# Slot logits one iteration later, and the copies of the transposed x ahead of the copies of the scores

## The chip, the cores and the metric

One core of a Trainium2 chip runs the whole program. The metric is the device time of one execution in microseconds (us), median over the runs; lower is better.

## The reference, cut to what matters

Three layers follow one another: windowed attention with four sink tokens, a soft mixture of experts, and a dense layer with the activation h - tanh(h).

```python
B, H, S, D = 4, 8, 768, 64              # 4 batches, 8 heads, 768 tokens
scores = q @ k.T / sqrt(D)              # kept where key < 4 or 0 <= i - j < 128
a = exp(scores - max); a /= sum(a) + 1e-9
x = concat over heads of (a @ v)        # 3072 x 512
logits = x @ phi                        # 3072 x 32 slots
d = softmax of logits over the tokens   # dispatch
c = softmax of logits over the slots    # combine
slot_input = d.T @ x                    # 32 x 512
slot_out = per expert: relu(slot_input @ w1[e]) @ w2[e]     # 8 experts
y = c @ slot_out
h = y @ w_in; out = (h - tanh(h)) @ w_out
```

## The kernel before

The order of all instructions is written out by hand: each engine runs its own queue in the order in which the program emits. The program has three parts: a software-pipelined loop over attention, a drain that finishes attention and the dispatch sums, and then the experts and the dense layer, whose order a planner works out from estimated costs. Only the first two parts are touched.

**The loop.** Its iterations i = 0 to 47 stand for 4 batches b, 4 pairs of heads p and 3 parts m (i % 3) of four score tiles each. An iteration holds work of several stages at once. In the order of emission:

- x_task (L655) transposes two thirds or one third of an earlier pair's output on TensorE (L434, tile mi) and leaves its copy back to SBUF in the list held.
- trans(i - 4) (L731) transposes the normalised scores (tile pT), and VectorE multiplies them by masks (L741 to L749).
- exps(i - 2) (L696): ScalarE takes four exponentials with their sums (L702).
- conv_step: a conversion of weights on VectorE, ScalarE (L130) and GpSimd, in part of the iterations.
- do_logits (L796): the slots' logits of a pair of heads, six matmuls x phi (L449, tile mi) and one VectorE operation that stores or adds them in ls (L452 for the first pair of a batch, L454 after that).
- scores(i) (L659): sixteen matmul records (L672) into two of the three buffers of tile sc.
- copies(i) (L675): ScalarE copies the scores to Z (L686), twice, or once where m is 0 (there VectorE does the other half, L683); VectorE overwrites masked parts (L687) and takes the maxima (L693).
- norm(i - 2) (L707): a VectorE reciprocal (L709) and a GpSimd multiply (L712).
- x_out (L651): ScalarE copies what held has (L436), so as to free the tile mi.
- run_task: a step of the dispatch sums of a finished batch (L463, L471, L502, L512, L521, L530, L535, each with a tile mi).
- avs(i - 5) (L751): the products with v (L767); where m is 2 ScalarE copies the result to xt (L781, L782), from which logits and transposes read.
- another run_task, and some DMA issues on SyncE.

Tile mi has two buffers, sc three, pT one, Z five. An entry for the logits falls due LD iterations after the avs that completes the pair, one for the transposes XD iterations after (and the second transposes no earlier than the iteration after the first). With LD = 1 the logits of a pair stand in the next iteration, i % 3 = 2; transposes stand in iterations of any remainder, since those of batches 1 and 2 wait until the dispatch sums of the batch before are done, and then one follows in each iteration.

**The drain** begins when the loop has ended. It clears the list lq, in which nothing is left, and then emits t_ext, trans, avs and the rest in an order given by the string DRAIN, the logits of the last two pairs under the names lg2 and lg3 among it. The weights of the experts are loaded by SyncE into buffers that the loop has used, so those loads are released by the last reads of the loop and the drain.

Of the kernel before, what the change touches and what calls it, by code (L numbers as in the profile page):

```python
# [44 lines left out]
NF = 0  # L45
ZO = 2
WT = (0, 0)
LD, XD, LP = 1, 2, 0
R78 = (41, 42)
NE_, NK = 12, 6  # L50
WF = (2, 0, 0, 0, 3, 0)
# [182 lines left out]
def tile_kernel(ctx: ExitStack, tc: tile.TileContext, qk, vv, v0, v0t, nw, phi, w1, w2,  # L234
# [17 lines left out]
    def run(ctx, fast):  # L252
# [49 lines left out]
        def win_src(i):  # L302
            d, f = divmod(i, 4)
            return w_in[P * d:P * d + P, 512 * f:512 * f + 512]
# [47 lines left out]
        def attention(fast):  # L352
            nqk = {}
            with ExitStack() as c2:
                ap = c2.enter_context(tc.tile_pool(name="ap", bufs=1))

                def load_qk(i):
                    a = sv(7 + i % 2, 0, QK)
                    SP.dma_start(a, qk[i // NP_, i % NP_])
                    nqk[i] = [a, None]  # L360
# [45 lines left out]
                def misc():  # L406
                    tag = seq.pop(0) if seq else "mi"
                    return pp.tile([P, 512], F32, name=tag, tag=tag, bufs={"mi": 2, "sc": 3, "pT": 1, "av0": 1}[tag])
# [35 lines left out]
                def logits(b, p):  # L444
                    if p == 0:
                        ls[b] = ap.tile([G3, 256], F32, name="ls", tag="ls", bufs=2)
                    m = misc()
                    for q in range(3):
                        PE.matmul(m[NS * q:NS * q + NS, 0:256], phi_t[:, p, :],  # L449
                                  xT[b, p][:, 256 * q:256 * q + 256], start=True, stop=True)  # L450
                    if p == 0:
                        DVE.tensor_copy(ls[b], m[0:G3, 0:256])  # L452
                    else:
                        DVE.tensor_tensor(ls[b], ls[b], m[0:G3, 0:256], op=ALU.add)  # L454
# [184 lines left out]
                steps, xq, lq = [], [], []  # L639
                cur = [[]]  # L640

                def next_step():
                    cur[0] = list(steps.pop(0)) if steps else []

                def run_task():
                    if cur[0]:
                        cur[0].pop(0)()
# [3 lines left out]
                def x_out():  # L651
                    while held:
                        held.pop(0)()

                def x_task():  # L655
                    if xq and not held and xq[0][0] <= now[0] and xq[0][1] <= done[0]:
                        xq.pop(0)[2]()
# [17 lines left out]
                def copies(i):  # L675
                    pb, m = divmod(i, 3)
                    Z = Zs[i]
                    for u in range(2):
                        s = sc_t[i][u]
                        z = Z[:, 2 * u:2 * u + 2, :]  # L680
                        base = bass.AP(s.tensor, s.offset, [list(s.ap[0]), [268, 2], [1, 132]])
                        if m == 0 and u == 0:
                            DVE.tensor_tensor(z, base, c_t[:, C_AB:C_AB + 264].rearrange("p (a c) -> p a c", a=2),  # L683
                                              op=ALU.add)
                        else:
                            ACT.copy(z, base)  # L686
                            DVE.copy_predicated(bass.AP(z.tensor, z.offset, [list(z.ap[0]), [196, 2], [1, 64]]),  # L687
                                                c_t[:, C_CM:C_CM + 128].bitcast(U32).rearrange("p (a c) -> p a c", a=2),
                                                bass.AP(s.tensor, s.offset + 132, [list(s.ap[0]), [68, 2], [1, 64]]))
                        if m == 0 and u == 1:  # L690
                            DVE.tensor_tensor(z[:, 0, 128:132], s[:, 128:132], c_t[:, C_C:C_C + 4], op=ALU.add)
                    mx = ap.tile([P, 4], F32, name="mx", tag="mx", bufs=4)
                    DVE.tensor_reduce(mx, Z, axis=AX.X, op=ALU.max)  # L693
                    small[i] = mx
# [36 lines left out]
                def trans(i, tag="pT"):  # L731
                    Z = Zs.pop(i)
                    pt = pp.tile([P, 512], F32, name=tag, tag=tag, bufs=1 if tag == "pT" else 3)
                    for u in range(4):
                        PE.transpose(pt[:, P * u:P * u + P], Z[:, u, 0:P], ident)  # L735
                    pb, m = divmod(i, 3)
                    src = pt.rearrange("p (t c) -> p t c", t=2)
                    mL, mU = (bass.AP(c_t.tensor, c_t.offset + o, [list(c_t.ap[0]), [0, 2], [1, 256]])
                              for o in (C_ML, C_MU))
                    if m == 0:  # L740
                        DVE.tensor_tensor(lu(0)[:, 256:512], pt[:, 256:512], mU[:, 0, :], op=ALU.mult)  # L741
                    elif m == 1:
                        d = sv(10, 512, 1024).rearrange("p (t l c) -> p t l c", t=2, l=2)
                        DVE.tensor_tensor(d[:, :, 1, :], src, mU, op=ALU.mult)
                    else:
                        for t in range(2):
                            DVE.tensor_tensor(lu(3 + t)[:, 256:512], src[:, t, :], mU[:, t, :], op=ALU.mult)
                    d = (sv(10, 1024 * m, 1024) if m < 2 else sv(11, 0, 1024)).rearrange("p (t l c) -> p t l c", t=2, l=2)
                    DVE.tensor_tensor(d[:, :, 0, :], src, mL, op=ALU.mult)  # L749
# [46 lines left out]
                def do_logits():  # L796
                    if lq and lq[0][0] <= now[0]:
                        logits(*lq.pop(0)[1:])


                def filler(s, n):
                    for _ in range(n):
                        PE.matmul(s[:, 400:512], z_t[:, 0:P], z_t[:, 0:112], start=True, stop=True)  # L803
# [29 lines left out]
                for i in range(NQ):  # L833
                    now[0] = i
                    next_step()
                    k = i - LAG
                    x_task()
                    if k >= 0:
                        trans(k)
                    k -= 1  # L840
                    if i >= 2:
                        exps(i - 2)
                    while stage[0] < min(3 * NC + 1, (i - 2) * CVR):
                        conv_step(stage[0])
                        stage[0] += 1
                    if LP == 0:
                        do_logits()
                    scores(i)
                    if i < NQ - 3:
                        filler(sc_t[i][1], NE_ if i < NK else NF)  # L850
                    copies(i)
                    if i == NQ - 1:
                        exps(NQ - 2)
                    if LP == 1:
                        do_logits()
                    if i % 3 == 2:
                        pre_dma = i // 3 + 2
                        if pre_dma < B * NP_:
                            load_qk(pre_dma)
                        else:  # L860
                            ring_dma(pre_dma - B * NP_ + 10)
                    if i >= 2:
                        norm(i - 2)
                    for b in range(B - 1):
                        if i in (12 * b + 14, 12 * b + 15):
                            sinks(b, (i % 12 - 2,))
                            break
                    else:
                        if gq:
                            gq.pop(0)()  # L870
                    if i == NQ - 1:
                        exps(NQ - 1)
                        norm(NQ - 2)
                    x_out()
                    if i < NQ - 1:
                        run_task()
                    if k >= 0:
                        avs(k)
                        if k % 3 == 2 and k // 3 + 2 < B * NP_:
                            load_v(k // 3 + 2)  # L880
                    run_task()
                    if i % 3 == 1 and pre:
                        ring_dma(pre.pop(0))
                    if i % 3 == 0 and i // 3 < 16 - NC:
                        SP.dma_start(late_raw(NC + i // 3), win_src(NC + i // 3))
                    for j, w in zip((5, 6), R78):
                        if i == w:
                            issued.add(j)
                            ring_dma(j)
# [16 lines left out]
                def warm_(n):  # L906
                    t = pp.tile([P, 512], F32, name="pT", tag="pT", bufs=1)
                    for _ in range(n):
                        PE.matmul(t[:, 0:ZN], z_t[:, 0:P], z_t, start=True, stop=True)

                lq.clear()
                t_ext, t_slota, t_slotb, t_slots, t_slotc = late2
                t_pst, t_sink, t_max, t_exp, t_trd, comb_max, t_ext2, t_trl, comb_sum, s_part, s_acc = tail_tasks(B - 1)[0]
# [1062 lines left out]
```

## Time and profile before

| what | value |
|---|---|
| median of 3 runs | 507.75 us (507.4 to 510.46) |
| the profiled execution | 508.94 us |
| its span, first to last instruction | 507.0 us |
| mean granted TensorE clock | 0.994 |
| TensorE busy | 480.7 us, 95% |
| VectorE busy | 414.6 us, 82% |
| ScalarE busy | 385.9 us, 76% |
| GpSimd busy | 301.6 us, 59% |

So 1.94 us of the profiled execution lie outside the span, and it is 1.19 us over the median. Shares are means over parts with different limits.

### The profile page before, as it was taken

Reading aid. Unit: us, or ns where it says so; the run is one execution under the profiler, and the core shown is the slowest. Engines: PE = TensorE matmul, PEld = TensorE weight load, DVE = VectorE, ACT = ScalarE, POOL = GpSimd, SP = SyncE. Lnnn points to the kernel's source line nnn. Section 1 sums busy time; section 2 is a strip of 40 time slices with the busy share of each in tenths; the row PEclk is TensorE's granted clock in tenths of the full one; section 3 lists DMA queues with packets and bytes.
Section 4 is the critical chain, followed back from the end, with each engine's and each line's share of the span. In section 5 each row is a group of like instructions: output and inputs, shape, how many; then the busy total and the mean of one; then the engine's idle time right before and its main releaser. Section 6 shows DMA issues by size and latency. Waiting matters only on the chain.

```text
span 507.0 us, 10286 instructions
## 1 busy us (share of the span) xinstructions
PE 480.7 (95%) x3558; PEld 336.7 (66%) x3558; DVE 414.6 (82%) x826; ACT 385.9 (76%) x1084; POOL 301.6 (59%) x366
## 2 busy tenths in 40 slices
PE   8799999899998999798999999999999999999995
PEld 4565655555555633235688888888888888888884
DVE  2999998998998559659999999788858798965892
ACT  4889998998999414337898987998768998855750
POOL 0466755765654100005899998358747794789871
PEclk9999999999999999899999999999999999999998
DMA  8989976532385999994433000220000030100022
GB/s 298 414 332 349 348 300 244 178 132 95 106 296 185 307 313 404 410 406 154 124 100 109 1 0 2 83 84 1 1 0 0 2 125 1 41 2 0 1 85 87
DMA packets 22139, 77.60 MB, mean 153 GB/s; under 512 B 2882, under 2 KB 4034, under 8 KB 20162
## 3 DMA queue, kind: packets, MB, share of 16 engines
q1 hardware_dynamic: 22082, 76.89, 41.4%
q8 instruction: 29, 0.48, 0.4%
q14 instruction: 28, 0.23, 0.1%
HBM read 70.59 MB, written 6.29 MB: 152 GB/s over the span
## 4 chain that ended last, share of the span: by engine, by line
PE 66%; DVE 10%; ACT 10%; DMA 8%; POOL 3%; issue 2%; DVEq 0%; POOLq 0%; SPq 0%; ACTq 0%
PE o L1507 44%; DMA w<-in_w 4%; ACT w L702 4%; PE sc L672 3%; PE o L1088 3%; PE av L767 2%; DMA w<-in_qk 2%; PE h L1576 2%; ACT w L686 2%; DVE mx L693 2%; DMA w<-in_w_out 2%; PE pT L735 2%; DVE w L749 1%; PE mi L530 1%; POOL gl L1320 1%
## 5 line engine op out<-in xcount | busy, mean ns | idle before, releaser
L1507 PE MATMUL o<-gh,whi 128*128 128x512 f32 x232 | 91.2, 393 | 0.0
L1507 PE MATMUL o<-gh,wlo 128*128 128x512 f32 x232 | 90.9, 392 | 0.0
L712 POOL TENSOR_TENSOR w<-w,su 128x528 f32<-128x528 f32 x38 | 40.6, 1068 | 52.4 <-DVE su L709 37.5
L1507 PE MATMUL o<-gl,whi 128*128 128x512 f32 x232 | 71.6, 390 | 0.0
L1499 POOL TENSOR_TENSOR gl<-w,gh 128x512 fp32r<-128x512 f32 x39 | 51.3, 1322 | 26.5 <-ACT gh L1645 15.5
L702 ACT ACTIVATE w<-w,nb 128x132 f32<-128x132 f32 x152 | 59.6, 393 | 1.2
L1507 PEld LDWEIGHTS o<-gh,whi 128*128 128x128 f32 x232 | 43.7, 188 | 9.9 <-ACT mk L1705 0.2
L1507 PEld LDWEIGHTS o<-gh,wlo 128*128 128x128 f32 x232 | 43.6, 188 | 9.7
L1507 PEld LDWEIGHTS o<-gl,whi 128*128 128x128 f32 x232 | 43.6, 188 | 9.5
L767 PE MATMUL av<-w,w 128*64 128x256 f32 (+1 forms) x448 | 48.3, 344 | 0.0
L672 PE MATMUL sc<-w 64*64 64x200 f32 (+2 forms) x768 | 44.8, 331 | 2.3 <-DMA w<-in_qk 1.4
L1147 POOL TENSOR_SCALAR whi<-wx 128x512 fp32r<-128x512 f32 x6 | 3.7, 619 | 62.8 <-DMA w<-in_w_out 61.0
L767 PEld LDWEIGHTS av<-w,w 128*64 128x64 f32 x448 | 25.8, 136 | 16.4 <-issue 10.7
L672 PEld LDWEIGHTS sc<-w 64*64 64x64 f32 x768 | 26.1, 132 | 15.1 <-issue 9.9
L1334 DVE TENSOR_TENSOR h<-u,h 128x512 f32<-128x512 f32 x40 | 27.6, 691 | 10.0 <-ACT u L1588 9.9
L1645 ACT CAST gh<-h 128x512 fp32r<-128x512 f32 x40 | 23.6, 590 | 11.1 <-DVE w L1499 4.2
L749 DVE TENSOR_TENSOR w<-pT,c_t 128x512 f32<-128x512 f32 x46 | 31.3, 680 | 0.0
L1645 ACT CAST gh<-w 128x512 fp32r<-128x512 f32 x39 | 24.2, 621 | 7.9 <-PE o L1507 7.6
L686 ACT COPY w<-sc 128x264 f32<-128x264 f32 x63 | 21.1, 373 | 11.9 <-PE sc L803 6.1
L1499 DVE TENSOR_TENSOR gl<-h,gh 128x512 fp32r<-128x512 f32 x40 | 27.4, 685 | 2.7 <-ACT gh L1645 2.0
L702 ACT ACTIVATION_READ_ACCUMULATOR w<-w,nb 128x1 f32 x152 | 28.3, 186 | 0.0
L693 DVE TENSOR_REDUCE mx<-w 128x4 f32<-128x528 f32 x38 | 26.7, 703 | 1.3
(388 smaller groups left out, 1332.2 us busy)
## 6 DMA issues: line engine op xcount, KB each, us to landing
w<-in_w SPq DMA_DIRECT2D x30, 512.0 KB, 10.2
w<-in_w SPq DMA_DIRECT2D x14, 1024.0 KB, 6.5
w<-in_qk SPq DMA_DIRECT2D x16, 780.0 KB, 6.1
w<-in_w_out SPq DMA_DIRECT2D x16, 512.0 KB, 3.6
w<-in_vv SPq DMA_DIRECT2D x16, 384.0 KB, 4.0
w<-in_w_in SPq DMA_DIRECT2D x8, 512.0 KB, 4.8
out<-xt SPq DMA_DIRECT2D x12, 256.0 KB, 2.0
win_t<-in_w_in SPq DMA_DIRECT2D x4, 512.0 KB, 9.5
```

The lines of the kernel that those rows point to most:

```text
L672: PE.matmul(sc_t[i][u][w, o:o + n], a[r, 64 * j:64 * j + 64], kslc(a, lo, n)[r, :], start=True, stop=True)
L686: ACT.copy(z, base)
L693: DVE.tensor_reduce(mx, Z, axis=AX.X, op=ALU.max)
L702: ACT.activation(Z[:, u, :], Z[:, u, :], AF.Exp, bias=nb[:, u:u + 1], scale=SCALE, accum_out=su[:, u, :])
L712: (POOL if i < NQ - 1 else DVE).tensor_tensor(Z, Z, su.to_broadcast([P, 4, CH]), op=ALU.mult)
L749: DVE.tensor_tensor(d[:, :, 0, :], src, mL, op=ALU.mult)
L767: PE.matmul(dst[r, :], v[:, t, r], l, start=start, stop=stop, skip_group_check=True)
L1088: PE.matmul(ha[x][NS * g:NS * g + NS, :], sT[f // 2][:, f % 2, :], ring_t(i + g, o, 512), start=f == 0, stop=f == 3)
L1334: DVE.tensor_tensor(g, u, h, op=ALU.mult)
L1499: td.any_of(at, {e: (us[e], lambda e=e: names[e].tensor_tensor(dst, a, b, op=alu), len(engs) > 1 or sbuf) for e in engs}, rd, wr)
L1507: PE.matmul(o, w, a, start=start, stop=stop)
L1645: add(at, "ACT", US["cast"], [gn], [f"gh{x}"], lambda: ACT.copy(gh_b[x], g))
```

## The change

Four edits. LD goes from 1 to 2: the logits of a pair are computed one iteration later, at i % 3 = 0 instead of 2. The call of x_out moves from behind norm and sinks to the place in front of copies, so that ScalarE's queue holds the copy of the transposed x ahead of the copies of the scores of the same iteration. As the pair (3, 1) is now due after the last iteration, a loop in front of lq.clear() computes what lq still holds for pairs under 2, at the head of the drain. Nothing else differs.

```diff
-LD, XD, LP = 1, 2, 0
+LD, XD, LP = 2, 2, 0
...
                     if i < NQ - 3:
                         filler(sc_t[i][1], NE_ if i < NK else NF)
+                    x_out()
                     copies(i)
...
                     if i == NQ - 1:
                         exps(NQ - 1)
                         norm(NQ - 2)
-                    x_out()
                     if i < NQ - 1:
                         run_task()
...
+                for a in lq:
+                    if a[2] < 2:
+                        logits(*a[1:])
                 lq.clear()
```

## Rows read from the trace of the kernel before

**Rows 1.** Stretches of the run: each engine's busy time (instructions), granted clock, DMA share, GB/s

```profile
29.00:163.00 134.00, 125.83 (x1495) 76.79 (x1494) 123.63 (x328) 126.58 (x547) 83.92 (x121) 1.00 0.63 229
163.00:182.00 19.00, 18.45 (x202) 11.44 (x202) 11.46 (x33) 8.55 (x28) 3.66 (x13) 1.00 0.90 318
182.00:196.00 14.00, 13.61 (x124) 4.25 (x128) 9.97 (x21) 3.21 (x5) 0.00 (x0) 1.00 0.96 335
196.00:228.00 32.00, 27.69 (x201) 10.61 (x197) 21.18 (x41) 12.61 (x24) 0.00 (x0) 0.95 1.03 408
```

**Rows 2.** Shorter stretches of the loop, the same columns

```profile
29.00:56.00 27.00, 25.54 (x297) 15.92 (x296) 25.16 (x67) 26.43 (x117) 18.66 (x25) 1.00 0.87 322
...
83.00:99.00 16.00, 14.82 (x176) 9.24 (x173) 15.71 (x40) 15.71 (x67) 10.35 (x20) 1.00 0.46 141
...
146.00:163.00 17.00, 15.24 (x186) 9.18 (x177) 15.22 (x42) 16.08 (x71) 6.54 (x11) 1.00 0.59 202
```

**Rows 3.** The chain that ended last, in order of time: start, length, what

```profile
129.08 0.56 PE mi L449 x6
...
130.56 0.66 ACT w L686 x2
131.22 0.50 ACT x L436
131.76 0.44 PE mi L434 x2
...
138.47 1.67 ACT w L702 x8
...
157.90 0.42 DVE w L687 x2
...
196.28 10.94 DMA w<-in_w
```

**Rows 4.** Waits, 15 to 172 us: who for whom, us in total, times, longest

```profile
DVE w L687 <- ACT w L686: 4.5, 11, 0.7
...
PE mi L449 <- ACT xt L781: 1.7, 3, 0.7
...
PE mi L512 <- ACT x L436: 1.3, 2, 0.9
PE mi L434 <- ACT x L436: 0.7, 1, 0.7
```

**Rows 5.** The instructions of one line, with their durations in ns

```profile
L436 ACT COPY x<-mi x24: 371/482/603, 34.3 to 154.1; 128x512 f32<-128x512 f32 x12, 128x256 f32<-128x256 f32 x12
...
  PE sc L434: 2.1, 1
  PE pT L434: 0.3, 1
```

**Rows 6.** The timeline at four places: start, duration, engine, line, idle before

```profile
99.56 0.58 DVE L687 COPY_PREDICATED w<-c_t,sc 128x128 f32<-128x128 uint32 x2 [0.68 <-ACT w L686]
99.70 0.39 ACT L436 COPY x<-mi 128x256 f32<-128x256 f32 x1
99.96 0.23 ACT L698 ACTIVATE nb<-mx 128x4 f32<-128x4 f32 x1
...
113.59 0.20 PEld L512 LDWEIGHTS mi<-c_t,ls 96*128 96x128 f32 x2 [1.36 <-ACT x L436]
...
130.56 0.66 ACT L686 COPY w<-sc 128x264 f32<-128x264 f32 x2 [0.40 <-PE sc L672]
...
154.27 0.30 DVE L687 COPY_PREDICATED w<-c_t,sc 128x128 f32<-128x128 uint32 x1 [0.39 <-ACT w L686]
```

**Rows 7.** The end of the loop, VectorE and ScalarE

```profile
160.16 0.66 ACT L686 COPY z<-sc 128x264 f32<-128x264 f32 x2 [0.25 <-PE sc L672]
...
160.22 0.41 DVE L454 TENSOR_TENSOR ls<-ls,mi 96x256 f32<-96x256 f32 x1
160.57 0.58 DVE L687 COPY_PREDICATED z<-c_t,sc 128x128 f32<-128x128 uint32 x2
```

## The prediction

> **What bounds the kernel now.** I read the busy times by stretch first, since the shares of the whole run mix three parts. In the loop, from 29 to 163 us, three engines are near full at once: of 134.00 us ScalarE is busy 126.58, TensorE 125.83, VectorE 123.63 [rows 1]. So none has more than some 10 us to give back, and ScalarE, the fullest, has 134.00 - 126.58 = 7.42 us. In two stretches it is the bound by itself: 26.43 of 27.00 us from 29 to 56, and 15.71 of 16.00 from 83 to 99 [rows 2]. There no order of its queue can gain more than 0.57 and 0.29 us.
>
> Second, the chain that ended last, which tells whose wait ends last at each place. It runs through ScalarE in those two stretches, through TensorE at 129 to 132 us, through VectorE near the loop's end, and at 196 us it steps into a transfer of weights [rows 3]. From 163 to 182 us, the drain, TensorE is busy 18.45 of 19.00 us; from 196 to 228 us the DMA engines are full, a share of 1.03 at 408 GB/s [rows 1]. Those transfers go to buffers that loop and drain set free, and the stream still has gaps from 163 to 182 us (a share of 0.90), so an earlier end of the loop moves the whole stream; a gain made only after 182 us would not.
>
> Third, the waits. The change can end three sorts of TensorE idle time: logits that wait for ScalarE's copy of the pair's output, 1.7 us, and matmuls that wait for a copy of x out of tile mi, 1.3 and 0.7 us [rows 4]; in all 3.7 us in the loop. Against them stands one wait that the change can lengthen: VectorE's masked overwrite waits for ScalarE's copy of the scores, 4.5 us in 11 places [rows 4].
>
> **The change, part by part.** No instruction is added or removed. What moves: 24 copies of x, twelve of four blocks and twelve of two, 371 to 603 ns each [rows 5], and the logits of 14 pairs, six matmuls and one VectorE operation each. The four-block copy holds up ScalarE's queue by 0.50 us [rows 3]; the two-block copy by 99.96 - 99.70 = 0.26 us, the time to the start of its successor [rows 6]. Neither part issues a DMA. The copies of x pass only copies of scores on ScalarE's queue; the logits pass one iteration's scores, products and maxima on TensorE's and VectorE's queues; GpSimd's and SyncE's queues stay as they are.
>
> *Logits one iteration later.* In the chain at 129 to 132 us logits of 0.56 us stand right in front of scores for which ScalarE has idled 0.40 us [rows 3, 6]. Moved, they let the scores end 0.56 us earlier, of which ScalarE can take the 0.40 us in which it sat idle: **-0.40 us**. They come back in the next iteration, in front of its scores; ScalarE has an iteration's exponentials, 1.67 us [rows 3], to take before it wants those, so I cost the return at nothing. If that cover fails the return costs 0.56 us, and the part is +0.16. The 1.7 us that TensorE waits for the pair's output end too, but in the timeline they stand at 38, 48 and 97 us, in the two stretches in which ScalarE is the bound: TensorE will wait elsewhere, and I take 0 of them (bounds 0 and -1.7).
>
> *The end of the loop.* The logits of pair (3, 1) leave the last iteration for the head of the drain. Their VectorE operation stands there directly ahead of the masked overwrite, 160.22 to 160.57, and the chain passes through VectorE just ahead of it at 157.90 [rows 3, 7]. ScalarE's copy of these scores started at 160.16 after idling 0.25 us for them, with the same logits in front of them; so both feeders of the overwrite come earlier, and it can start 0.35 us earlier: **-0.35 us**. The six matmuls, 0.56 us, come back at the drain's head. TensorE has 163.00 - 146.00 - 15.24 = 1.76 us idle from 146 to 163 us [rows 2], so I cost them at nothing; uncovered, they cost +0.56 in a drain in which TensorE is 97% busy.
>
> *Copies of x in front: what is gained.* At 113.59 us a transpose of the dispatch sums waits for a copy of x that stands behind one copy of scores; TensorE's weight load waited 1.36 us [rows 6]. The copy of x can start one copy of scores earlier, which as its own spacing shows is worth about 0.26 us: **-0.26 us**, with the other such waits, 1.3 + 0.7 - 0.9 us, as the bound beyond. Where ScalarE idles for scores a copy of x fills the gap: at 130.56 this is the same 0.40 us already counted, so it is not added.
>
> *What is lost.* In front of the masked overwrite ScalarE now does a copy of x first. Where VectorE already waits for ScalarE, the overwrite starts later by the whole copy, 0.26 us at 99.56 and 0.26 us at 154.27 [rows 6], both with a two-block copy and both in places where VectorE is on or near the chain: **+0.52 us**. Elsewhere VectorE reaches the overwrite after the copy has ended, or the chain lies on ScalarE, where the order does not matter: 0. For all eight copies that I count in the stretches where the chain is VectorE's (three of 0.50, five of 0.26) the bound is 1.50 + 1.30 = +2.8 us.
>
> The Trainium skill (PSUM — Partial Sum Buffer, section Engine vs sequencer instructions) says that ScalarE's queue is strict first in, first out. By it the edit could stall ScalarE outright, if scores were ready and the transposes ahead of them were not. The trace speaks against it: the waits of a copy of x for its transposes, 2.1 and 0.3 us, are for tiles sc and pT [rows 5], that is, the drain's; none is for mi, the loop's.
>
> *The sum.* -0.40 - 0.35 - 0.26 + 0.52 = -0.49 us on the profiled execution: 508.94 - 0.49 = 508.45. That execution is 1.19 us over the median of the runs, so the median would be 507.75 - 0.49 = 507.26; I take **507.2 us**.
>
> **Rivals.**
>
> *Score copies held up (slower).* If VectorE is the pace in more of the loop than I read, each copy of x in front delays overwrite, maxima and, through the three sc buffers, the next scores. The price is 0.50 or 0.26 us per copy, and it decides where VectorE arrives less than that after ScalarE's copy ends. With the eight copies above, and the gains kept: -0.40 - 0.35 - 0.26 + 2.8 = +1.8, 509.5 us. With all 24 copies, 12 x 0.50 + 12 x 0.26 = +9.1 us, the gains left aside: 516.9 us. For it: the 11 waits of 4.5 us, VectorE's 123.63 of 134 us. Against: the exponentials that use a maximum stand two iterations behind it, so that 1.67 us of other exponentials [rows 3] lie between.
>
> *Smoother than I read (faster).* All 3.7 us of TensorE's waits on xt and x go, with the 0.40 and 0.35 us: 507.75 - 4.45 = 503.3 us. For it: TensorE is 94% busy and each of its stalls is followed by others'. Against: in ScalarE's stretches there is nothing to give, and 7.42 us of its idle time is the ceiling for the whole loop.
>
> *Nothing that reaches the end.* The loop ends earlier and the transfers don't, as loads already queue back to back from 163 us on; or the waits named move to the normalised scores, for which TensorE waits as well. Time 507.75 us. The Trainium skill (Perfetto Trace Analysis, section Roofline) puts the ceiling of one core's sixteen DMA engines at about 435 GB/s. The trace's 408 GB/s is close under it, so by this rule that stretch itself cannot shrink; only its start can move.
>
> **How the numbers follow.** A per cent, 5.1 us, is about what a measurement can tell from no change. My forecast, a gain of some tenths up to 2 us, gets 0.53; nothing reaching the end 0.15; the slower rival 0.18, of which 0.05 beyond 512.8 us; the faster one 0.14, of which 0.06 beyond 502.7 us, as that needs over two thirds of ScalarE's idle time. Slower by over 1%: 0.05 plus 0.01 for an unseen wait, 0.06; faster: 0.06; between: 0.88. The range runs from the faster rival's price to a little over the slower rival's first price, 503.3 to 510.3 us, and leaves out about 0.17.
>
> **What would show it.** In the profile after: no wait of logits for xt; transposes that wait for a copy of x at less than 1 us in all; at the scores in front of which the logits stood, ScalarE without its 0.40 us; and the wait of the masked overwrite for ScalarE risen from 4.5 us by some 0.5 to 1.5 us. The loop's end, the last GpSimd multiply of the loop and the first full stretch of DMA should all move by the same tenths. The prediction is wrong if that wait rises by 3 us or more, if TensorE starts to wait for tile sc, or if the busy share of ScalarE from 29 us to the loop's end rises by over two points.

## The result: 0.8% slower

The changed kernel takes 511.52 us against 507.40 us, medians of five runs each: a ratio of 1.0079, 95% interval [1.0055, 1.0103]. Forecast was a small gain, 507.2 us, in a range from 503.3 to 510.3 us; the kernel became slower, and its time lies above the range. Of all runs below one, of the change with the logits in their own place behind the scores, took 664.53 us at a granted clock of 0.656, and its ratio leaves that run out.

The profiled execution after has a span of 510.6 us, 3.6 us more than before. The same kind of stretches, moved by the 3.7 us by which the loop now ends later, answer to [rows 1]:

```profile
29.00:166.70 137.70, 126.21 (x1495) 76.42 (x1494) 124.55 (x326) 127.12 (x547) 84.31 (x121) 1.00 0.63 224
166.70:185.70 19.00, 18.28 (x201) 11.22 (x201) 11.53 (x34) 8.54 (x28) 3.67 (x13) 1.00 0.85 299
185.70:199.70 14.00, 13.59 (x123) 4.34 (x126) 9.90 (x22) 3.21 (x5) 0.00 (x0) 1.00 0.96 334
199.70:231.70 32.00, 26.46 (x201) 10.63 (x193) 21.39 (x40) 12.28 (x23) 0.00 (x0) 1.00 1.03 408
```

The work is the same (TensorE 126.21 us against 125.83, ScalarE 127.12 against 126.58), but the loop needs 137.70 us for it: ScalarE's idle time rose from 7.42 to 10.58 us, TensorE's from 8.17 to 11.49. Everything behind the loop only starts later. So the loss is waits inside the loop. The list of waits from 24 to 170 us answers to [rows 4]. For ScalarE's wait for scores the same list of the kernel before has

```profile
ACT w L686 <- PE sc L672: 3.3, 5, 1.3
```

and the changed kernel has

```profile
ACT w L686 <- PE sc L672: 8.2, 8, 1.9
DVE w L687 <- ACT w L686: 5.5, 11, 0.9
PE mi L449 <- DVE pst L464: 2.5, 3, 0.9
PE mi L434 <- ACT x L436: 2.4, 4, 0.9
PE mi L502 <- ACT x L436: 2.2, 2, 1.2
...
PE mi L471 <- ACT x L436: 0.2, 1, 0.2
```

The 1.7 us of logits waiting for xt are gone, as forecast. In their place the logits (L449) wait for the copy of pst, a step of the dispatch sums, three times, and transposes (L434, and L502 of the dispatch sums) wait longer for a copy of x. All three waits are for a buffer of tile mi: its two buffers are taken in turn, as a ring, and who takes one next waits until its last reader is done. ScalarE pays in turn: it waits for scores 8.2 us.

The timeline of the changed kernel (start, duration, engine, line, idle before) shows one such place, TensorE first, then VectorE, and after that the loop's end:

```profile
58.12 0.44 PE L463 MATMUL mi<-c_t,skn 128*96 128x128 f32 x2
58.49 0.65 PE L767 MATMUL av<-w,w 128*64 128x256 f32 x4
59.07 0.66 PE L434 MATMUL mi<-c_t,xt 128*128 128x128 f32 x4
59.83 0.66 PE L735 MATMUL pT<-c_t,w 128*128 128x128 f32 x4
61.16 0.63 PE L449 MATMUL mi<-xt,phi_t 128*32 128x256 f32 x6 [0.68 <-DVE pst L464]
61.72 0.90 PE L672 MATMUL sc<-w 64*64 64x132 f32 x16
62.78 0.63 PE L471 MATMUL mi<-pst,R 32*32 32x128 f32 x12 [0.16 <-ACT x L436]
...
60.01 0.70 DVE L693 TENSOR_REDUCE mx<-z 128x4 f32<-128x528 f32 x1
60.72 0.39 DVE L464 COPY pst<-mi 96x256 f32<-96x256 f32 x1
...
163.80 0.21 ACT L704 ACTIVATE su<-su 128x4 f32<-128x4 f32 x1
163.91 0.64 ACT L686 COPY z<-sc 128x264 f32<-128x264 f32 x2
...
164.31 0.58 DVE L687 COPY_PREDICATED z<-c_t,sc 128x128 f32<-128x128 uint32 x2 [0.68 <-ACT z L686]
```

At 58.12 pst takes one mi buffer, at 59.07 a transpose of x the other. The logits, which now come next, need the first back, and its reader on VectorE stands behind the maxima until 60.72. TensorE's matmuls run here in the order of the program, so the scores behind the logits wait too, until 61.72. In the kernel with the copies of x alone (the second experiment) the same stretch has no logits between, and the scores go out 1.4 us earlier, of which 0.68 us are the wait and 0.56 us the logits' own time (61.16 to 61.72):

```profile
59.28 0.65 PE L434 MATMUL mi<-c_t,xt 128*128 128x128 f32 x4
59.77 0.60 PE L735 MATMUL pT<-c_t,w 128*128 128x128 f32 x4
60.30 0.90 PE L672 MATMUL sc<-w 64*64 64x132 f32 x16
61.13 0.63 PE L471 MATMUL mi<-pst,R 32*32 32x128 f32 x12
```

At this place ScalarE still had other work and did not idle for the late scores. Two later places show the price. At 102.63 us the same order of maxima, copy of pst, logits and scores stands on the chain that ended last (first four lines: start, length, what), and ScalarE then idles for the scores (last line, from the timeline):

```profile
101.48 0.70 DVE mx L693
...
102.27 0.32 DVE pst L464
...
102.63 0.63 PE mi L449 x6
103.27 0.83 PE sc L672 x14
...
104.20 0.38 ACT L686 COPY w<-sc 128x264 f32<-128x264 f32 x1 [0.58 <-PE sc L672]
```

The same chain passes the same steps at 144.92 us, and at 115.04 and 157.33 us transposes (L502) that waited 1.04 and 1.21 us for a copy of x.

### The profile page after: what moved, and what is told of

The parts are those of the page before. It is cut to its first block, busy times and chain, and to the rows that moved or that the text cites. A ratio compares the mean times of both kernels' runs of the same rounds, so it can differ in the third digit from the quotient of the medians.

```text
span 510.6 us, 10280 instructions
## 1 busy us (share of the span) xinstructions
PE 479.5 (94%) x3558; PEld 336.4 (66%) x3558; DVE 415.7 (81%) x826; ACT 386.1 (76%) x1084; POOL 301.7 (59%) x366
## 4 chain that ended last, share of the span: by engine, by line
PE 65%; DMA 13%; ACT 11%; DVE 6%; POOL 2%; issue 1%; SPq 1%; POOLq 0%; DVEq 0%; ACTq 0%
PE o L1510 44%; DMA w<-in_w 8%; ACT w L702 5%; PE av L767 5%; PE sc L672 3%; DMA w<-in_qk 2%; PE h L1579 2%; PE pT L735 2%; DMA w<-in_w_out 2%; DMA w<-in_vv 1%; PE mi L530 1%; POOL gl L1323 1%; ACT w L686 1%; DVE mx L693 1%; PE y L1579 1%
```

## The experiments

Differences in us are the ratio less one, times 507.5 us, against the kernel before, timed beside it. Their intervals reach from 0.5 to 1.2 us to either side; a difference of two rows is less certain than either.

| kernel | median, us | ratio to before, interval | difference |
|---|---|---|---|
| the change | 511.52 | 1.0079 [1.0055, 1.0103] | +4.0 |
| later logits only | 513.05 | 1.0104 [1.0089, 1.0120] | +5.3 |
| copies of x only | 507.01 | 0.9988 [0.9979, 0.9997] | -0.6 |
| change, logits behind scores | 515.97 | 1.0158 [1.0140, 1.0176] | +8.0 |
| change, logits two iterations later | 514.71 | 1.0139 [1.0123, 1.0154] | +7.1 |
| change, last pairs' logits not moved | 510.10 | 1.0056 [1.0038, 1.0073] | +2.8 |
| copies, and last pairs' logits moved | 510.85 | 1.0065 [1.0044, 1.0086] | +3.3 |
| change, dispatch steps later too | 512.56 | 1.0097 [1.0081, 1.0112] | +4.9 |
| change, pst copied by ScalarE | 511.35 | 1.0077 [1.0061, 1.0092] | +3.9 |
| change, logits in a place of their own | 508.33 | 1.0009 [0.9996, 1.0022] | +0.5 |
| copies, own place, old iteration | 506.69 | 0.9976 [0.9964, 0.9988] | -1.2 |
| copies, own place, two later | 524.12 | 1.0314 [1.0293, 1.0335] | +15.9 |
| change, own place, behind scores | 508.59 | 1.0013 [0.9999, 1.0027] | +0.7 |
| copies, own place, VectorE's part later | 508.10 | 1.0009 [1.0000, 1.0018] | +0.5 |

**Which half.** Theory A blames the later logits, theory B the copies of x, as my slower rival did. The first kernel has LD = 2 and the drain's loop, with x_out in its old place; the second is the kernel before with x_out moved (its call behind norm and sinks is gone):

```diff
                         filler(sc_t[i][1], NE_ if i < NK else NF)
+                    x_out()
                     copies(i)
```

> The logits one iteration later, with the copies of x in their old place behind the copies of the scores. Theory A (crowded tile mi: the later logits share an iteration with a transpose of x and a step of the dispatch sums, three users of two buffers, and TensorE's in-order queue passes their waits on to the scores): nearly the whole loss stays, 3 to 5 us over the kernel before, and the waits of the logits for the copy of pst (2.5 us in 3 places in the changed kernel) stay. Theory B (the copies of x hold up the copies of the scores, the slower rival of the prediction): within 1 us of the kernel before.

> Copies of x ahead of the copies of the scores, with the logits in their old iteration. Theory A: within 1 us of the kernel before, rather under it, as transposes that wait for a copy of x wait less. Theory B: 3 to 5 us over it, with the wait of VectorE's overwrite for ScalarE's copies well over 4.5 us.

A holds on the time and B falls: the later logits alone cost 5.3 us, a little more than the 3 to 5 us of A, and the copies alone gain 0.6 us. In the waits of the copies' kernel VectorE's overwrite waits less than before, not more:

```profile
ACT w L686 <- PE sc L672: 4.3, 6, 1.3
DVE w L687 <- ACT w L686: 4.1, 10, 0.7
PE mi L434 <- ACT x L436: 0.2, 1, 0.2
```

One detail of A was off: without the early copies the logits wait 0.7 us for pst, not 2.5; the wait falls on the users behind them:

```profile
PE mi L434 <- ACT x L436: 4.4, 6, 1.1
PE mi L471 <- DVE ls L454: 1.8, 3, 1.1
PE mi L449 <- DVE pst L464: 0.7, 1, 0.7
```

**Where in the iteration, and how much later.** Two edits of one number each in the changed kernel (the comments, here and below, are not in the program):

```diff
-LD, XD, LP = 2, 2, 0
+LD, XD, LP = 2, 2, 1     # logits behind the scores
+LD, XD, LP = 3, 2, 0     # logits two iterations later
```

> The whole change, but in its iteration the logits are issued behind the scores instead of ahead of them. Theory A: what hurts is that the logits' own 0.56 us and their waits for a buffer stand ahead of the scores on TensorE; behind them ScalarE gets its scores on time: at least 2 us of the 4 us come back, and ScalarE's wait for scores falls from 9.9 us back towards 4.7. Theory B: unchanged, 3 to 5 us over the kernel before, as the copies stand where they stood.

> The whole change, but the logits two iterations later instead of one (LD = 3), so that they stand in the iteration with i % 3 = 1. Theory A: the loss depends on which steps meet in one iteration; that iteration has the longest products with v ahead of it but no step of the dispatch sums that waits for pst; 1 to 5 us over the kernel before, and other than the 4.1 us of the change. Theory B: the same 3 to 5 us as with LD = 2, within 0.7 us.

Both cost more than the change and more than either theory allowed. So A's picture that the logits merely stand in front of the scores was wrong: behind the scores, VectorE reads the logits' buffer behind the maxima as well, so it is held longer. The users that follow the logits in the ring now wait for that reader, and ScalarE's wait for scores does not fall (8.3 and 2.4 us, for tiles w and z, against 8.2 and 1.7):

```profile
PE mi L512 <- DVE ls L452: 2.2, 3, 1.5
PE mi L434 <- DVE ls L454: 1.4, 3, 0.6
```

**Which pairs.** In lq.append, and for the second with LD = 1 and the early copies:

```diff
-lq.append((i + LAG + 1 + LD, b, p))
+lq.append((i + LAG + 1 + (1 if p == NP_ - 1 else LD), b, p))   # last pair as before
+lq.append((i + LAG + 1 + (2 if p == NP_ - 1 else LD), b, p))   # last pair alone later
```

> The whole change, but the last pair of each batch keeps its logits in the old iteration; the other three pairs go one iteration later. Theory C (the loss is made where the last pair's logits meet the steps pst and sink of its batch: four users of the two mi buffers in one iteration, three times in the run): within 0.8 us of the kernel with the copies of x alone, so -1.5 to +0.5 us against the kernel before. Theory D (each moved set of logits costs its own some 0.3 to 0.4 us, since it lands in the iteration in which TensorE has most to do): three quarters of the loss stay, +2.5 to +3.5 us.

> Copies of x ahead as in the change; of the logits only the last pair's of each batch go one iteration later (three of fourteen moves). Theory C: nearly the whole loss with a fifth of the moves, +2.5 to +4.5 us over the kernel before. Theory D: a quarter of the loss, less the gain of the copies: 0 to +0.8 us.

Neither theory holds as put. Against the copies alone, the last pairs cost 3.9 us with three moves of fourteen, which D does not allow; the other pairs cost 3.4 us, which C does not. Together they cost 4.6, not 7.3. That the two groups' waits fall into the same idle time would explain it, but no run shows it.

**Which link.** One edit starts the dispatch steps an iteration later, the other lets ScalarE copy pst:

```diff
-steps.extend(a)
+steps.extend([[]] + a)
```
```diff
-DVE.tensor_copy(st["pst"][0:G3, :], m[0:G3, 0:256])
+(ACT.copy if b < B - 1 else DVE.tensor_copy)(st["pst"][0:G3, :], m[0:G3, 0:256])
```

> The whole change, and the steps of the dispatch sums of each batch begin one iteration later as well, so that the last pair's logits stand ahead of pst again, as in the kernel before. The transposes that wait for these sums move one iteration too. Theory C: the wait of the logits for pst's copy (2.5 us in 3 places) goes, and most of the loss with it, -0.5 to +1.5 us over the kernel before. Theory D: the loss stays, +3 to +5 us.

> The whole change, but the copy of pst out of tile mi is made by ScalarE instead of VectorE for the first three batches. Theory C with the wait for pst's copy as the link: the logits no longer wait for it, and 1 to 2.5 us of the 4.1 us come back, though ScalarE has 0.4 us more to do three times. Theory C with the crowd of buffers in general, or theory D: under 0.8 us come back, as the next user of mi waits in its place.

Both take away exactly the wait they aim at, and neither gains. With pst on ScalarE the logits no longer wait for it, but the step that uses pst (L471), 0.2 us in the change, now waits 2.8 us for a copy of x:

```profile
PE mi L471 <- ACT x L436: 2.8, 3, 1.1
PE mi L434 <- ACT x L436: 2.4, 4, 0.9
```

With the steps later, pst itself waits for a copy of x:

```profile
PE mi L463 <- ACT x L436: 3.5, 3, 1.4
```

So the wait for pst is not the cause by itself; when it is taken away, the next user of the ring waits instead. That led to theory E: the ring of two mi buffers.

**Logits out of the ring.** The tile av1 is 256 wide where the other PSUM tiles are 512. It is widened to 512 and allocated where it is first written, and the loop's logits go to its other half (do_logits passes own=True):

```diff
-                def logits(b, p):
+                def logits(b, p, own=False):
...
-                    m = misc()
+                    m = av[NP_ * b + p][1][:, 256:512] if own else misc()
...
-                                  pp.tile([P, 256], F32, name="av1", tag="av1", bufs=1))
...
+                    if m == 2:
+                        av[pb] = (av[pb][0], pp.tile([P, 512], F32, name="av1", tag="av1", bufs=1))
...
```

> The whole change, with the logits in the loop written to a place of their own (the unused half of the PSUM bank of av1, free between two pairs) instead of a buffer of tile mi; the rest of the order as in the change. Theory E (the ring of two mi buffers: the later logits stand between users that need the same buffers, and whichever user comes next waits for a reader on VectorE or ScalarE): with the logits out of the ring their place in the iteration hardly matters, -1.5 to +1 us against the kernel before, and within 1 us of the next kernel. Theory F (load: the logits' 0.56 us on TensorE and 0.35 us on VectorE land in the iteration that has most to do, ahead of its scores): +2.5 to +4.5 us stay.

> The same place of their own for the logits, with the copies of x ahead as in the change, but the logits in their old iteration. Theory E: about as the kernel with the copies of x alone, -2 to 0 us against the kernel before, as there the ring seldom bound; within 1 us of the kernel with the later logits in their own place. Theory F: the same -2 to 0 us here, but 3 us or more under that kernel.

> The logits in their own place and two iterations later (LD = 3), copies of x ahead. Theory E: -1.5 to +1.5 us against the kernel before, where the same order with the logits in tile mi cost 7.0 us. Theory F: +4 us or more, since the iteration with i % 3 = 1 has the longest products with v and the transposes as well.

E holds for most of it: later logits cost 4.6 us against old ones when they use mi (+4.0 against -0.6), and 1.7 us when they do not (+0.5 against -1.2), a little outside the 1 us that E allowed. In the waits of the change with the own place, ScalarE's wait for scores is back from 8.2 to 4.7 us and mi is hardly waited for:

```profile
DVE w L687 <- ACT w L686: 4.8, 8, 0.9
ACT w L686 <- PE sc L672: 4.7, 5, 1.9
PE mi L434 <- ACT x L436: 0.8, 2, 0.6
```

The third kernel misses E's forecast of at most +1.5 us by far, but says nothing on load: its edit made a wait of its own. The place must be read before av1 is written again, in the same iteration, and TensorE waited 13.8 us for that:

```profile
PE av L768 <- DVE ls L454: 9.3, 7, 2.0
PE av L768 <- DVE ls L452: 4.5, 3, 1.8
```

It is the same kind of wait on another buffer: logits moved up against the next use of the place that they take.

**The rest.** What the remaining 1.7 us are was asked twice: with LP = 1 in the change with the own place, and, in the fastest kernel, by holding back VectorE's operation alone until the next iteration's do_logits:

```diff
+                    if own:
+                        late_add.append(add)      # run at the head of the next do_logits
                     else:
...
+                        add()
```

> The logits one iteration later in their own place, copies of x ahead, and the logits issued behind the scores of their iteration instead of ahead of them. It asks what the 1.6 us are that later logits in their own place still cost over old logits in their own place. Theory F1 (the logits' 0.56 us of TensorE ahead of the scores of the fullest iteration): behind the scores they hold up nobody, -1.5 to 0 us against the kernel before. Theory F2 (VectorE: the operation that adds the logits lands in the iteration in which VectorE already has a third operation on the scores, wherever TensorE does its part): +0.3 to +1.5 us stay, or more, as VectorE's operation now also stands behind the maxima. With the logits in tile mi the same move made the change 4 us slower still; theory E expects that here it does not, since nobody waits for this place before the next pair's product with v.

> From the fastest kernel so far (logits in their own place and old iteration, copies of x ahead): TensorE's six matmuls stay there, and VectorE's operation that stores or adds them goes one iteration later alone, to where the change has it. Theory F2 (the residual 1.6 us of later logits in their own place are VectorE's): +0.2 to +1.0 us against the kernel before, 1.2 to 2 us over the kernel that it is made from. Theory F1 or G (the residual is TensorE's, or belongs to no single engine): -1.5 to -0.7 us, as the kernel that it is made from.

Behind the scores nothing comes back (+0.7, intervals overlapping), so TensorE's place ahead of the scores is not it, and, as E expected, the move that cost 4 us in tile mi costs nothing here. VectorE's part alone, with TensorE's left in place, costs as much as the whole residual (+0.5 against -1.2). The timeline of the kernel before suggests why that operation was free. These are overwrites in iterations with i % 3 = 2, in which the logits stood:

```profile
31.25 0.58 DVE L687 COPY_PREDICATED w<-c_t,sc 128x128 f32<-128x128 uint32 x2 [0.52 <-ACT w L686]
...
40.83 0.58 DVE L687 COPY_PREDICATED w<-c_t,sc 128x128 f32<-128x128 uint32 x2 [0.40 <-ACT w L686]
...
50.40 0.59 DVE L687 COPY_PREDICATED w<-c_t,sc 128x128 f32<-128x128 uint32 x2 [0.65 <-ACT w L686]
```

Seven of the eleven such waits fall in these iterations: VectorE had to wait for ScalarE there anyway, and 0.35 us of logits ahead of the wait (as from 160.22 to 160.57 in [rows 7]) cost nothing. In the next iteration VectorE also adds the mask to half the scores (L683) and seldom waits (two of the eleven). Held back, the operation leaves a hole. The wait is 4.0 us in the kernel without the edit (first line) and 5.5 us with it, where the lines of the program are numbered 7 higher:

```profile
DVE w L687 <- ACT w L686: 4.0, 10, 0.7
...
DVE w L694 <- ACT w L693: 5.5, 11, 1.0
```

## Why the prediction was wrong, point by point

- *Logits later, -0.40 us; their return "at nothing".* This is the step that failed: +5.3 us were measured with the logits moved alone, +4.6 us on top of the copies. The 0.40 us of ScalarE did go at the place named (its copy of those scores, at 133.22 us in the changed kernel, has no idle time before it), but the return was not free. I asked what covers 0.56 us of TensorE and did not follow the two resources that the logits bring along. The buffer of tile mi, whose next users I did not list, makes up about 2.9 us of the 4.6 (4.6 - 1.7, if the two parts add); the VectorE operation, which I moved without asking what it had hidden behind, the 1.7 us. Even the bound of this part, +0.16 us, took the return at TensorE's 0.56 us alone. The waits for xt did end; what that was worth by itself no run shows.
- *End of the loop, -0.35 us.* It did not come. In the changed kernel VectorE waits 0.68 us for ScalarE's copy at 163.91, which follows ScalarE's own work without a gap: the other feeder was the later one by then.
- *Copies of x in front, -0.26 and +0.52 us.* Measured alone, -0.6 us: the sign of the sum was wrong. The loss did not come, the overwrite waits 4.1 us instead of 4.5. TensorE's waits for copies of x fall from 2.0 to 1.1 us in all; at 130 us, where ScalarE idled 0.40 us for scores, the copy of x now fills the gap and the transposes behind it no longer wait. Over the loop ScalarE does not wait less for scores, though (4.3 us against 3.3). That no copy of x would wait for its transposes in the loop was right for this change: such waits are again 2.1 and 0.3 us, in the drain. The Trainium skill (PSUM — Partial Sum Buffer, section Engine vs sequencer instructions) states the strict order of ScalarE's queue by which such a stall could come. In the kernel with the logits behind the scores it came once, 0.4 us.
- *Slower rival.* Its sign came true by another mechanism: VectorE's overwrite did rise to 5.5 us, but with the later logits, not the copies.
- *What shows it.* Transposes waiting for a copy of x at under 1 us was wrong (2.4 + 2.2 us); that the loop's end would carry everything behind it was right: 3.7 us at the last maximum, 3.6 us in the span. None of the three signs of being wrong came: the overwrite's wait rose by 1.0 us and not by 3, the list of waits has none of the scores' matmuls for tile sc, and ScalarE's busy share fell, from 94.5% to 92.3%. They watched the copies of x, and no sign watched tile mi.
- *Nothing that reaches the end.* The stretch at 408 GB/s has 408 GB/s after the change too. That it "cannot shrink" was put too strongly, though, as the ceiling named there lies above this figure.

The fastest kernel of the study takes the copies from the change, leaves the logits where they were and gives them a place of their own: 506.69 us, ratio 0.9976 [0.9964, 0.9988]. That is faster than the kernel before and the changed one; against the copies alone (0.9988) the intervals overlap, so what the own place adds there is not shown.

## What to carry to other kernels

Moving a step moves its place in the ring of every buffer that it takes: list the users of that ring in the new order, and for each the reader on which the next one will wait, before pricing the step itself. An operation that is free ahead of a wait need not be free one iteration later, so ask of each part of a moved step which wait hid it. If removing one wait gains nothing and the next user shows the same time, suspect the number of buffers; taking one user out of the ring is a test. A third buffer for mi, the direct test, was not tried here.

## What was not expected

When ScalarE copied pst, the wait moved whole: 2.5 us of the logits became 2.8 us of the step after them. Costs were not additive: 3.9 and 3.4 us for the two groups of pairs, 4.6 us for both.
